# Shorter expert choice, another order of attention's steps and gates from gathered logits in a WKV and two-layer mixture-of-experts kernel

## The chip, the cores and the metric

The kernel runs on one core of a Trainium2 chip. The metric is the device time of one execution in microseconds (us); several runs are given as their median. A profile is one further execution, with every instruction's start and duration.

## The reference

Inputs are r, k, v, w of shape (2, 8, 768, 48), u, two gate matrices and two sets of expert weights (8 experts, 384x1024 and 1024x384). All arithmetic is float32.

```python
for t in range(S):                      # attention, per batch and head
    y[:, :, t] = r_t @ (state + u*k_t (x) v_t)
    state = w_t[:, None] * state + k_t (x) v_t
x = y as (1536, 384)
# layer one
logits = x @ w_gate + modality_bias[modality_id]
e = argmax(logits); gate = softmax(logits)[e]      # sum + 1e-9
x = gate * (relu(x @ w1[e]) @ w2[e])
# layer two: the same without bias; an expert takes its first 384 tokens only, others give 0
```

## The kernel before, in words

**Attention** (`attention`, L192 on) works on eight pairs of heads, i = 0 to 7, each in six chunks of 128 tokens; g = 6i + chunk counts chunks from 0 to 47. Per pair: `turn` transposes w, k, r (PE) and ACT or DVE evacuates them; `scan_s` and `scan_j` (DVE) make the decay products S and J; `mul_r` multiplies rT by J on DVE or POOL, as the string MR says by pair (L297); `uterm` and `uterm2` make the u term on POOL and DVE; `front` makes the masked scores of two chunks (PE, then `Am` on DVE, L376); `state` carries the 112x112 state: a matmul of keys and values, and then either the old state is added through the identity on PE (STATE letter p) and ACT scales (L403), or DVE adds (Z, L398) and scales (X, L401; letter v). `out_y` makes the output. The score tile in PSUM has one buffer and `Am` three.

The order is written out by hand: each engine runs its instructions in the order in which they are issued. PLAN gives, for each pair, the position (in thirds of a chunk) at which each of its steps is issued; PRE and PLAN0 do so for pair 0; FRONT, PRE, PLAN0 and END place fillers, matmuls on a constant whose result is not used (L524); XTURN, XTURN2 and XLOG place the transposes of the output and the logits of layer one; SLOT places constants, stores and the choice.

**Choice of experts** (`Pick.find`, L140 to 184). After the first batch's six chunks of logits, a count of tokens per expert is made, and the two experts with most tokens are searched, twice over with max, comparison, scan and mask. Their numbers go to registers of the SP queue, which then loads these two experts' weights. One step is issued every half chunk (`pull`), from SLOT["pick"] on. The order of the others follows (`hop`, `upto`).

**Routing** (`routing`, L771 on). From the one-hot choice of all tokens, DVE and PE make a place for every token: blocks of 256 tokens of one expert, each of two tiles of 128; `ids` and `idg` hold the token of each place. `sub`, `ex` and later `gates`, `gates1`, `gates2` (L912 to 931) make the softmax weight of each token and bring it to its place with 12 matmuls (pg, L928).

**A layer** (`moe`, L997 on) goes over the blocks. Block j gathers the rows of block j + 2 (POOL, L1046), loads the weights of block j + 2 (SP), casts the next block's weights into a high part on ACT (`hi`) and a rest on DVE (`lo`) (L1004, L1007), and runs three matmuls per product (L1080, L1115, L1128, L1146). `two` serves a block with two full tiles, `one` a block with one; which of them runs is an If on a register. In `one`, the strings of ONE say which casts and transposes are issued between the matmuls: a letter a to j is a weight piece, x and X transposes of the next block's rows, s the scaling, y, z and l the next layer's logits. In layer one each finished tile also gets its logits for layer two: with `yturn` and `ylog` in float32 for tile 0 of a two-tile block (L700, L710), and with `yturn3`, `ysplit3` and `ylog3` from three bf16 parts (L1165, L736) elsewhere. `scale` multiplies by the gate on ACT (s, L1152) or DVE (v, L1154), as SCALE says; `own` (block 0) places the rest of its weights' subtractions and the gates. `last` (L1343 on) ends layer one. The first expert of layer two is loaded ahead into the slot of the weights that is free; `p0` are the ten pieces of a layer's block 0, cast and subtracted at the layer's start. Here layer one has eight blocks (six of two tiles, two of one) and layer two ten (two, one, one, four of two, one, one, two).

## Time and profile before

| | |
|---|---|
| median of 3 runs | 474.61 us (472.51 to 476.15) |
| the profiled execution | 473.01 us |
| its span, first to last instruction | 471.3 us |
| mean granted clock of TensorE | 0.951 |
| busy, share of the span | PE 91%, PEld (weight loads) 83%, DVE 74%, ACT 51%, POOL 32% |
| attention, to the first routing | 0 to 128.8 us |
| routing and first gathers of layer one | 128.8 to 142.3 us |
| blocks of layer one | 142.3 to 290.1 us |
| end of layer one, routing of layer two | 290.1 to 308.9 us |
| blocks of layer two | 308.9 to 460.8 us |

How to read it: the profiled execution's own time is 1.7 us longer than its span. Engines are PE (TensorE), PEld (its weight loads, beside the matmuls), DVE (VectorE), ACT (ScalarE), POOL (GpSimd), SP (SyncE, which only issues transfers). A granted clock of 1.00 is the 2.4 GHz level of TensorE, 0.50 the level of 1.2 GHz. In a timeline row the bracket gives the idle time of the engine before the instruction and what ended it; x3 means three instructions in a row. Matmul ends are modelled. Instructions on one engine overlap at their ends, so a row may start before the one above it has ended.

### The profile page before, as it was taken

The page shows a single profiled execution, that of the slowest core. Times are in us where ns is not written, and L with a number is a line of the kernel's source. Part 1 is how long each engine was busy: PE and PEld are TensorE (multiplying, and loading weights), DVE is VectorE, ACT ScalarE, POOL GpSimd, SP SyncE. Part 2 cuts the span into 40 slices and gives each one's busy share as a digit, 9 for nine tenths or more (in the row PEclk, how much of TensorE's full clock was granted, in tenths as well). Part 3 has the DMA queues.
Part 4 walks back from the last instruction along what each step waited for, and adds up shares of the span by engine and source line. Part 5 has one row for each costly group of instructions (what it writes and reads, how often), then busy time and mean ns, then how long its engine had stood idle before and what let it go on. Part 6 is the DMA issues. An engine that isn't in the chain of part 4 may idle for free. (4 is left out here: it accounts for less than half of the span.)

```text
span 471.3 us, 9450 instructions
## 1 busy us (share of the span) xinstructions
PE 429.7 (91%) x3188; PEld 389.5 (83%) x3188; DVE 346.9 (74%) x669; ACT 239.4 (51%) x472; POOL 150.3 (32%) x159
## 2 busy tenths in 40 slices
PE   7989999979979899999999787898999999999990
PEld 4778878868739899999999776388899999998990
DVE  7787977994288984865947587889989559569770
ACT  3335353522344473654745464545857547568560
POOL 5528767230032032021220331243533221224500
PEclk9979999995799999999999889899999999999996
DMA  6966538108632022137772763431597676684200
GB/s 114 200 110 121 100 60 202 30 2 329 230 110 69 2 69 73 37 106 223 259 231 74 208 207 117 160 87 35 206 312 269 203 232 234 184 250 130 54 10 25
DMA packets 83989, 66.82 MB, mean 142 GB/s; under 512 B 58986, under 2 KB 76055, under 8 KB 83904
## 3 DMA queue, kind: packets, MB, share of 16 engines
q1 hardware_dynamic: 78912, 52.26, 37.4%
q0 software_dynamic: 4992, 13.53, 10.1%
q8 instruction: 42, 0.69, 0.6%
q14 instruction: 43, 0.35, 0.2%
HBM read 95.55 MB, written 11.51 MB: 227 GB/s over the span
## 5 line engine op out<-in xcount | busy, mean ns | idle before, releaser
L1007 DVE TENSOR_TENSOR w1l<-w1r,w1h 128x512 fp32r<-128x512 f32 x120 | 75.2, 683 | 0.8 <-ACT w1h L1004 0.7
L1007 DVE TENSOR_TENSOR w2l<-w2r,w2h 128x768 fp32r<-128x768 f32 x80 | 71.9, 949 | 0.7 <-ACT w2h L1004 0.5
L1004 ACT CAST w1h<-w1r 128x512 fp32r<-128x512 f32 x120 | 66.2, 621 | 7.2 <-DMA w2r<-in_moe_w_dram 6.2
L1004 ACT CAST w2h<-w2r 128x768 fp32r<-128x768 f32 x80 | 61.5, 838 | 0.0
L1133 ACT ACTIVATE qhh_m<-qh_m 128x512 fp32r<-128x512 f32 x48 | 28.7, 599 | 62.5 <-PE qh_m L1128 58.9
L1134 DVE SCALAR_TENSOR_TENSOR qhl_m<-qh_m,qhh_m 128x512 fp32r<-128x512 f32 x48 | 32.9, 686 | 28.4 <-ACT qhh_m L1133 27.8
L1128 PE MATMUL qh_m<-xh,w1h 128*128 128x256 f32 x288 | 51.6, 288 | 0.5 <-PE lpl_y_m L710 0.3
L1157 POOL DMA_INDIRECT x<-yo,ids_l x14 | 15.1, 1080 | 115.6 <-DVE yo L1154 66.0
L1128 PE MATMUL qh_m<-xl,w1h 128*128 128x256 f32 x288 | 50.2, 283 | 0.1
L1128 PE MATMUL qh_m<-xh,w1l 128*128 128x256 f32 x288 | 49.8, 282 | 0.0
L1157 POOL DMA_INDIRECT out_dram<-yo,ids_l x20 | 24.9, 1244 | 67.7 <-DVE w1l L1007 17.8
L1128 PEld LDWEIGHTS qh_m<-xh,w1h 128*128 128x128 f32 x288 | 42.3, 188 | 1.1 <-ACT xh L1337 0.8
L1046 POOL DMA_INDIRECT xg<-x,idg_l x24 | 28.1, 1170 | 45.8 <-PE xp_m L1061 32.4
L1128 PEld LDWEIGHTS qh_m<-xl,w1h 128*128 128x128 f32 x288 | 41.0, 189 | 0.5 <-DVE w2l L1007 0.5
L1128 PEld LDWEIGHTS qh_m<-xh,w1l 128*128 128x128 f32 x288 | 40.9, 188 | 0.0
L403 ACT ACTIVATE X<-endt,Sb 112x112 f32<-112x112 f32 x32 | 11.3, 354 | 50.9 <-PE endt L393 37.2
L1046 POOL DMA_INDIRECT xg<-xs,idg_l x20 | 22.7, 1136 | 34.9 <-DVE ec_l L888 29.1
L418 PE MATMUL py<-raw_v,Am 128*128 128x96 f32 x192 | 32.7, 299 | 0.0
L1062 ACT CAST xh<-xp_m 128x384 fp32r<-128x384 f32 x38 | 16.7, 485 | 27.9 <-PE xp_m L1061 26.6
L418 PEld LDWEIGHTS py<-raw_v,Am 128*128 128x128 f32 x192 | 29.5, 220 | 0.1
L1146 PE MATMUL qy_m<-w2h,qhh_m 128*128 128x384 f32 x96 | 25.6, 348 | 0.0
L1146 PE MATMUL y_m<-w2h,qhh_m 128*128 128x384 f32 x96 | 25.1, 342 | 0.0
(281 smaller groups left out, 964.7 us busy)
## 6 DMA issues: line engine op xcount, KB each, us to landing
w2r<-in_moe_w_dram SPq DMA_DIRECT2D x50, 768.0 KB
w1r<-in_moe_w_dram SPq DMA_DIRECT2D x72, 512.0 KB
xs<-zv SPq DMA_DIRECT2D x12, 192.0 KB
out_dram<-zt SPq DMA_DIRECT2D x4, 576.0 KB
raw_w<-in_w_dram SPq DMA_DIRECT2D x14, 144.0 KB
raw_r<-in_r_dram SPq DMA_DIRECT2D x14, 144.0 KB
raw_k<-in_k_dram SPq DMA_DIRECT2D x14, 144.0 KB
raw_v<-in_v_dram SPq DMA_DIRECT2D x14, 144.0 KB
```

The costliest lines, as they stand in the source:

```text
L403: nc.scalar.activation(Xn, z, AF.Identity, scale=Tn)
L418: nc.tensor.matmul(py[:, 1 - h : 4 - h : 2, 0:D], lhsT=Am[:, h], rhs=vc[:, ch, :, 0:D], start=not ch, stop=True, skip_group_check=True)
L1004: (eng.copy if eng is nc.scalar else eng.tensor_copy)(p[1], p[0])
L1007: eng.tensor_sub(p[2], p[0], p[1].bitcast(F32))
L1046: nc.gpsimd.indirect_dma_start(out=m.xg[j % 2][:, t, 0:SW], out_offset=None, in_=src, in_offset=bass.IndirectOffsetOnAxis(ap=R.idg[:, 2 * ...
L1062: nc.scalar.copy(m.xh[j % 2][:, :, ts], pt)
L1128: nc.tensor.matmul(ph[:, f], lhsT=w[s][:, kc, fs], rhs=a[s][:, kc], start=(i == 0), stop=(i == 3 * KD - 1))
L1133: nc.scalar.activation(hh, ph, AF.Relu)
L1134: nc.vector.scalar_tensor_tensor(hl, ph, 0.0, hh.bitcast(F32), ALU.max, ALU.subtract)
L1146: nc.tensor.matmul(st["y", j, t], lhsT=a[:, f, ts], rhs=w[s][:, 2 * q + f], start=(q == 0 and i == 0), stop=(q == 3 and i == 5))
L1157: nc.gpsimd.indirect_dma_start(out=dst, out_offset=bass.IndirectOffsetOnAxis(ap=R.ids[:, 2 * j + t : 2 * j + t + 1], axis=0), in_=m.yo[j % ...
```

## The change

- **Choice of experts.** `find` makes one key, 8 times the count plus the expert's number, and takes the two largest and their indices with `max` and `max_index`. It is issued from SLOT["pick"] = 32 instead of 27.
- **Attention.** All of PLAN, PRE, PLAN0, FRONT, MR, STATE, SLOT, XTURN and XTURN2 are new: STATE has p at all five places, MR gives pairs 2, 4, 5 and 6 to DVE, and the fillers are placed anew.
- **Routing.** `sub`, `ex`, `rk`, `sr` go; the place is (inc + s0) times the one-hot. The one-hot `ohp` is made in three pieces of 6, 4 and 2 columns instead of two of 6.
- **Gates.** The scratch xs gets 8 more columns, into which the logits of layer one are written; the gather brings them with the row, in layer two as before. In each block max, difference (DVE), exponential (ACT), sum and reciprocal (DVE) give the gate of its 256 places: `gates(j, 0)` and `gates(j, 1)`, issued for the next block.
- **Next logits.** Tile 0 of a two-tile block uses `yturn3`, `ysplit3`, `ylog3`; its transposes are issued one product earlier. In `one`, z and l are issued earlier.
- **Scaling** is on ACT everywhere.
- **First weights of layer two.** They are cast in the last block of layer one already, as its next block's; layer two no longer casts them again. Where the last block's number is even, `last` does it.

```diff
 WARM = (4, 12, 2, 15)
 TP = (3, 4)
+OHP = ((0, 6), (6, 10), (10, 12))
...
-PRE = ('F6', 'n0', 'w0', 'w1', 'F0', 'A', 'S0', 'J0', 'r0', 'F0', 'A', 'm0', 'k0', 'S1', 'F8', 'r1', 'F2', 'J1', 'm1', 'K0', 'F1', 'k1', 'F6')
-FRONT = {0: 3, 1: 6}
-PLAN0 = {0: ('F0', 'n1', 'K1', 'F0', 'u', 'F0'), 3: ('A',), 1: ('U',), 10: ('c0',), 14: ('c1',)}
-MR = 'vggggggg'
-STATE = 'pppvp'
+PRE = ('F6', 'n0', 'w0', 'w1', 'F5', 'A', 'S0', 'J0', 'r0', 'F0', 'A', 'm0', 'k0', 'S1', 'F5', 'r1', 'F3', 'J1', 'm1', 'K0', 'F5', 'k1', 'F0')
+FRONT = {1: 7, 13: 2, 20: 1}
+PLAN0 = {0: ('F2', 'n1', 'K1', 'F0', 'u', 'F2'), 3: ('A',), 1: ('U',), 10: ('c0',), 14: ('c1',)}
+MR = 'ggvgvvvg'
+STATE = 'ppppp'
...
-SLOT = {'consts': 21, 'small': 9, 'pick': 27, 'xs': 29, 'flag': 44}
+SLOT = {'consts': 17, 'small': 10, 'pick': 32, 'xs': 26, 'flag': 44}
...
-SCALE = 'vsv'
+SCALE = 'ssv'
...
-ONE = (('ecadfyb', '01z', 'X', '', 'lhgix', 'js'), ('badec0', 'f1h', 'xX', 'i', 'j', 'sg'))
+ONE = (('ecadfyz', '01b', 'X', 'l', 'hgixq', 'jsQ'), ('badec0', 'f1h', 'xX', 'qi', 'jQ', 'sg'))
...
+        with self.nc.allow_low_precision(reason="whole numbers up to six"):
+            ins = v.tensor_reduce(half, self.oh[:, :, 0:CH], AX.X, ALU.add)
...
+        yield v.scalar_tensor_tensor(n, pc, float(E), num, ALU.mult, ALU.add)
+        yield v.max(top, n)
+        yield v.max_index(self.index, top, n)
+        yield v.tensor_copy(self.at, self.index[0:1, 0:2])
         yield "at"
...
+        yield v.tensor_scalar(self.force, n, top[:, 1:2], None, ALU.is_ge)
         key = T("key", [P, E])
-        yield v.tensor_sub(key, b, a)
+        yield v.tensor_scalar(key, n, top[:, 0:1], None, ALU.is_equal)
+        yield v.scalar_tensor_tensor(key, n, top[:, 1:2], key, ALU.is_equal, ALU.subtract)
...
+                nc.sync.dma_start(xs.rearrange("(c p) e -> p c e", p=P)[:, cols, DM:XW], lg[:, cols])
...
-        v.tensor_sub(sub, lg, mxb)
...
-        nc.scalar.activation(ex, sub, AF.Exp)
...
-        v.tensor_mul(rk, inc, oh)
...
-            v.scalar_tensor_tensor(rk, r1, cap[:, 0:1], rk, ALU.is_le, ALU.mult)
...
-        v.tensor_reduce(sr, rk.rearrange("p e c -> p c e"), AX.X, ALU.add)
...
-        v.tensor_tensor(so, oh, s0.unsqueeze(2).to_broadcast((P, E, NC)), ALU.mult)
+        v.tensor_tensor(so, inc, s0.unsqueeze(2).to_broadcast((P, E, NC)), ALU.add)
+        v.tensor_tensor(so, so, oh, ALU.mult)
...
-        v.tensor_add(sl, sl, sr)
...
-        for h in range(2):
...
+        for a, z in OHP:
+            v.tensor_tensor(ohp[:, :, a:z], c.i1[:, :, a:z], ps_[:, a:z].unsqueeze(1).to_broadcast((P, P, z - a)), ALU.is_equal)
...
-    for p in p0:
-        hi(p, nc.scalar)
     if layer == 0:
+        for p in p0:
+            hi(p, nc.scalar)
...
+        def gates(j, part):
+
+            gd = m.gd[j % 2]
+            if part == 0:
+                lx = m.xg[j % 2][:, :, DM:XW]
+                nc.vector.tensor_reduce(m.gm[:, 0], lx, AX.X, ALU.max)
+                nc.vector.tensor_tensor(gd[:, :, 0:E], lx, m.gm[:, 0].unsqueeze(2).to_broadcast((P, 2, E)), ALU.subtract)
+                nc.scalar.activation(gd[:, :, 0:E], gd[:, :, 0:E], AF.Exp)
+            else:
+
+                nc.vector.tensor_reduce(m.gm[:, 1], gd, AX.X, ALU.add)
+                nc.vector.reciprocal(R.gate[:, 2 * j : 2 * j + 2], m.gm[:, 1])
...
-            scale(j, 1, SCALE[2])
+            scale(j, 1, "s")
...
-            if j:
+            if j or layer:
                 split(pc, 0, 2)
...
+                gates(j + 1, 0)
             second2(j, 3, 0)
             scale(j, 0, SCALE[1])
...
+            if j + 1 < NU:
+                gates(j + 1, 1)
             second2(j, 1, 1)
+            if layer == 0:
+                yturn3(j, 0)
+                ysplit3()
             second2(j, 2, 1)
-            if layer == 0:
-                yturn(j, 0)
             second2(j, 3, 1)
             if layer == 0:
-                ylog(j, 0)
-            if layer == 0:
-                scale(j, 1, SCALE[2])
+                ylog3(j, 0)
+                scale(j, 1, "s")
...
-        for i in range(6):
+        for i in range(6) if layer == 0 else ():
             lo(p0[i], nc.vector)
...
+                if j % 2 == 0:
+                    for p in p0:
+                        hi(p, nc.scalar)
+                        lo(p, nc.vector)
...
-    xs = dr.tile([N, DM], F32, name="xs")
+    xs = dr.tile([N, XW], F32, name="xs")
```

## Rows read from the trace of the kernel before

**Rows 1.** Windows: length, busy PE, PEld, DVE, ACT, POOL, granted clock, DMA share, GB/s.
```profile
22.50:26.00 3.50, 0.50 (x6) 0.21 (x5) 3.46 (x5) 0.18 (x1) 1.68 (x1) 0.91 0.79 92
26.00:32.50 6.50, 6.40 (x33) 5.77 (x33) 5.01 (x8) 2.48 (x6) 1.15 (x1) 0.52 0.63 119
32.50:100.80 68.30, 65.15 (x663) 57.21 (x662) 57.93 (x104) 33.06 (x89) 39.60 (x51) 1.00 0.45 95
100.80:104.00 3.20, 0.94 (x11) 0.61 (x9) 3.17 (x8) 0.00 (x0) 2.94 (x3) 0.98 0.00 0
104.00:124.00 20.00, 19.72 (x109) 17.69 (x110) 8.33 (x29) 5.44 (x16) 1.15 (x1) 0.50 0.75 277
```

**Rows 2.** Timeline of PE: start, duration, idle before in brackets, releaser.
```profile
24.84 0.29 PE L391 MATMUL endt<-raw_v,KT 128*48 128x48 f32 x4 [2.12 <-DVE Z L398]
...
103.10 0.71 PE L373 MATMUL pa<-rT,kT 48*128 48x128 f32 x8 [2.08 <-DVE Am L376]
```

**Rows 3.** Timeline of DVE and POOL around the second pause.
```profile
99.26 1.71 POOL L297 TENSOR_TENSOR rT<-rT,Jf 112x768 f32<-112x768 f32 x1 [6.29 <-DVE pk_mx L156]
...
99.47 1.53 DVE L158 TENSOR_TENSOR_SCAN pk_cum<-first,pk_eq 128x8 f32<-128x8 f32 x1
...
100.93 1.40 POOL L321 TENSOR_TENSOR z<-raw_r,raw_k 128x576 f32<-128x576 f32 x1
...
101.26 1.10 DVE L159 SCALAR_TENSOR_TENSOR pk_one<-pk_cum,pk_eq 128x8 f32<-128x8 f32 x1
...
102.28 0.68 DVE L376 TENSOR_TENSOR Am<-pa,mask 128x512 f32<-128x512 f32 x1
```

**Rows 4.** Groups of lines on DVE, 0 to 128 us: busy, mean ns.
```profile
L401 DVE TENSOR_SCALAR X<-Z,Sb 112x112 f32<-112x112 f32 x8 | 6.4, 804 | 0.3
...
L398 DVE TENSOR_TENSOR Z<-endt,X 112x112 f32<-112x112 f32 x8 | 2.1, 268 | 4.4 <-PE endt L391 4.4
...
L297 DVE TENSOR_TENSOR rT<-rT,Jf 112x384 f32<-112x384 f32 x2 | 1.1, 558 | 0.2
```

**Rows 5.** Timeline of PE: nine fillers, and one addition of the old state.
```profile
10.46 2.11 PE L524 MATMUL junk<-fill 128*128 128x512 bf16 x9
...
45.29 0.45 PE L393 MATMUL endt<-X,ident 112*112 112x112 f32 x2
```

**Rows 6.** Timeline of PE: matmuls of the gates, layer one, then layer two.
```profile
155.61 0.87 PE L928 MATMUL pg_m<-rg_l,ohp_l 128*128 128x78 bf16 x12 [1.13 <-DVE rg_l L924]
...
322.14 0.89 PE L928 MATMUL pg_m<-rg_l,ohp_l 128*128 128x78 bf16 x12 [1.12 <-DVE rg_l L924]
```

**Rows 7.** Timeline of one full two-tile block of layer one: PE, DVE, ACT.
```profile
208.22 0.39 PE L736 MATMUL l_y_m<-wp,yp 128*128 128x24 bf16 x9
...
218.70 0.51 PE L1146 MATMUL qy_m<-w2h,qhh_m 128*128 128x384 f32 x2
...
221.13 0.73 PE L710 MATMUL lpl_y_m<-wg,lxT_y_m 128*128 128x8 f32 x6
...
216.99 1.02 DVE L1063 TENSOR_TENSOR xl<-xp_m,xh 128x384 fp32r<-128x384 f32 x2 [0.29 <-ACT xh L1062]
...
217.85 0.58 ACT L1152 ACTIVATE yo<-qy_m,gate_l 128x384 f32<-128x384 f32 x1 [0.52 <-PE qy_m L1146]
```

**Rows 8.** Timeline of PE, DVE and ACT around a one-tile block of layer two.
```profile
432.41 0.51 PE L1080 MATMUL ph_m<-w1h,xl 128*128 128x512 f32 x1 [0.51 <-DVE w2l L1007]
...
429.67 2.68 DVE L1007 TENSOR_TENSOR w2l<-w2r,w2h 128x768 fp32r<-128x768 f32 x3
...
428.19 2.33 ACT L1004 CAST w2h<-w2r 128x768 fp32r<-128x768 f32 x3
```

**Rows 9.** Timeline of DVE: a reduction in the routing of layer two.
```profile
299.06 0.31 DVE L834 TENSOR_REDUCE sr_l<-rk_l 128x12 f32<-128x96 f32 x1
```

**Rows 10.** Timeline of POOL and PE: the gather of layer two and its first block.
```profile
304.98 1.01 POOL L1046 DMA_INDIRECT xg<-x,idg_l  x1 [0.31 <-issue]
...
308.19 0.55 PE L1336 MATMUL xp_m<-ident,xg 128*128 128x128 f32 x3 [0.71 <-DMA xg<-x,idg_l]
```

More of the change, by code (lines that the diff above doesn't have):

```diff
@@ L135, in __init__ @@
         self.T = lambda nm, shape, dt=F32: g.tile(shape, dt, name="pk_" + nm)
-        self.one = []
         self.at = self.T("at", [1, 2])
-        self.ati = self.T("ati", [1, 2], I32)
+        self.index = self.T("index", [P, 8], mybir.dt.uint32)
+        self.ati = self.index.bitcast(I32)
     def find(self):
         v, c, T = self.nc.vector, self.c, self.T
-        n = T("n", [P, E])
-        yield v.tensor_reduce(n, self.oh[:, :, 0:CH], AX.X, ALU.add)
         half = T("half", [P, E], BF16)
-        yield v.tensor_copy(half, n)
+        with self.nc.allow_low_precision(reason="whole numbers up to six"):
+            ins = v.tensor_reduce(half, self.oh[:, :, 0:CH], AX.X, ALU.add)
+        yield ins
         yield
@@ L788, in routing @@
         oh = best.oh
-        mxb = best.mx.unsqueeze(2).to_broadcast((P, NC, E))
         inc = T("inc", [P, E, NC], BF16)
@@ L910, in places @@
             v.scalar_tensor_tensor(R.tc, ti, -float(NC), R.ids, ALU.mult, ALU.add)
-        def gates():
-            yield v.tensor_reduce(se, ex, AX.X, ALU.add)
-            yield v.tensor_scalar(se, se, 1e-9, None, ALU.add)
-            yield v.reciprocal(gt, se)
-            for i in range(3):
-                yield v.tensor_copy(g3[:, :, i], gt)
-                if i < 2:
-                    yield v.tensor_sub(gt, gt, g3[:, :, i])
-        def gates1():
-            for i in range(3):
-                yield v.tensor_tensor(rg[:, :, i], ohb, g3[:, :, i].unsqueeze(2).to_broadcast((P, NC, NB)), ALU.mult)
-        def gates2(pg):
-            for col in range(NC):
-                nc.tensor.matmul(pg, lhsT=ohp[:, :, col], rhs=rg[:, col], start=(col == 0), stop=(col == NC - 1))
-            v.tensor_copy(gs, pg)
-            v.tensor_add(gs[:, 0], gs[:, 0], gs[:, 1])
-            v.tensor_add(R.gate, gs[:, 0], gs[:, 2])
-        R.control, R.places, R.gates, R.gates1, R.gates2 = control, places, gates, gates1, gates2
+        R.control, R.places = control, places
     return R
@@ L994, in __init__ @@
         self.yp = cp.tile([P, 3, KD, P], BF16, name="yp")
+        self.gd = slots("gd", [P, 2, E + 1], F32)
+        self.gm = cp.tile([P, 2, 2], F32, name="gm")
 def moe(tc, c, m, route, run, layer, src, w1d, w2d, dst, wg2, wp2, zb, following, lgs=None, psum=None, bad=None, general=None):
@@ L999, in moe @@
     n = f"_m{layer}{run}"
-    SW = XW if layer else DM
     SO = DM if layer else XW
@@ L1191, in own @@
             if k < 2:
-                for i in (6 + 2 * k, 7 + 2 * k):
+                if k == 0:
+                    gates(0, 1)
+                for i in (6 + 2 * k, 7 + 2 * k) if layer == 0 else ():
                     lo(p0[i], nc.vector)
@@ L1195, in own @@
                     load(2, (1,))
-            elif k == 2:
-                for ops in (R.gates, R.gates1):
-                    for _ in ops():
-                        pass
-            else:
-                R.gates2(psum.tile([P, 3, NB], F32, tag="tp", name="pg" + n, bufs=TP[layer]))
-                if layer == 0:
-                    R.places()
+            elif layer == 0:
+                R.places()
         def one(j, pc):
@@ L1268, in two @@
             own(j, 1)
-            if j:
+            if j or layer:
                 split(pc, 2, 6)
@@ L1277, in two @@
             own(j, 2)
-            if j:
+            if j or layer:
                 split(pc, 6, 10)
@@ L1283, in two @@
             first2(j, 3)
-            if j == 0:
+            if j == layer == 0:
                 split(pc, 6, 8)
             second2(j, 1, 0)
-            own(j, 3)
             second2(j, 2, 0)
```

57 lines of the change are left out of this document (19 added, 38 removed).

## The prediction

> **What bounds the kernel now.** I read the windows first, then the timelines of PE and DVE at the places where the windows are thin, then the groups of lines. PE is the engine that ends last nearly everywhere: in the long middle of attention it is busy 65.15 of 68.30 us at a granted clock of 1.00 [rows 1], and in the two-tile blocks of both layers its matmuls follow each other without a gap. The exceptions are what this change can win. In attention there are two pauses. At 22.5 to 26.0 PE works 0.50 of 3.50 us, and the next 6.50 us run at 0.52, about the lower level of 1.2 GHz; at 100.8 to 104.0 it works 0.94 of 3.20 us, and the next 20.00 us run at 0.50 [rows 1]. Both pauses have one shape: a first wait of 2.12 and 2.08 us for DVE, once for the state's sum Z, once for the masked scores Am [rows 2]. DVE was not short of time on average; it was held. From 99.26 POOL multiplies (rT, then z). A DVE scan over 8 columns that starts at 99.47 ends at 101.00, just behind POOL's end at 100.97, and the next small one, 101.26 to 102.36, ends with POOL's second product at 102.33; Am comes only at 102.28 [rows 3]. Those two small instructions are part of the choice of experts.
>
> **Attention.** What the two pauses cost: idle 3.50 - 0.50 = 3.0 and 3.20 - 0.94 = 2.3 us. Work at the lower level: the middle stretch does 663 matmuls in 68.30 us, 9.7 per us; 33 matmuls would take 3.4 instead of 6.5 us, and 109 would take 11.2 instead of 20.0 [rows 1]. That is 3.1 and 8.8 us. Together 17.2 us, the ceiling of what the new layout can return.
>
> The first pause goes because the fourth state of a pair is no longer summed and scaled on DVE: STATE has no v left. DVE loses eight Z and eight X, 2.1 + 6.4 us busy [rows 4]. PE gains eight additions through the identity, at most 0.45 us each and less when they overlap [rows 5]; I take 0.28, in all 2.2 us. The eight scalings go to ACT, which is busy 33.06 of 68.30 us [rows 1]. The second goes because the choice now has 6 steps up to the index instead of 17, starts five chunks later, and has done its search (max, max_index) in chunk 37, before the product of the last pair is issued to POOL in chunk 38. What is added: six more fillers net (PRE 24 for 23, FRONT 10 for 9, PLAN0 4 for none), 2.11 / 9 = 0.23 us each [rows 5], 1.3 us as a bound since some fall into waits. So 17.2 - 2.2 - 1.3 = 13.7 us at best.
>
> The new order has its own danger. Four products rT*J move from POOL to DVE, at 2 x 0.56 = 1.1 us each [rows 4]; that of pair 6 stands behind a scan and two kT and in front of the next Am. Sums of DVE durations over such four-chunk stretches come to about 9 us, against about 8 us of PE. The first chunks can wait too: its transposes use three PSUM tiles, and one is freed only behind the scan J of pair 1. New pauses can cost from nothing to the whole 17.2; I take 5.0: one pause, a little less than the smaller of the two measured ones with its slow stretch (3.0 + 3.1). Attention: -17.2 + 3.5 + 5.0 = -8.7.
>
> The Trainium skill, "SBUF — State Buffer", section "Who interferes with whom", says that a DVE instruction with two SBUF inputs contends with a GpSimd instruction that reads SBUF, and that whichever is second is fully blocked. The held scan agrees [rows 3]. The rule speaks against MR: by it each moved product can be held for a POOL product, 4 x 1.40 = 5.6 us of DVE time more; no such product beside POOL is in this trace.
>
> **Routing.** On the path from logits to indices the reduction sr and the sum sl + sr go, and one sum of inc and s0 comes; in layer two the masking of rk, another pass over 96 columns, goes too. The removed reduction takes 0.31 us [rows 9]; I price the new sum and the mask like it, so that reduction and sum cancel, the narrow sum is worth 0.2, and the one-hots in 6, 4 and 2 columns leave two matmuls behind the last piece instead of six, another 0.2. The subtraction and rk itself stand beside PE's counts and cost nothing now. So -0.4 in layer one, -0.7 in layer two; between 0 and -1.5 for both.
>
> **Gates.** The matmuls pg disappear: wait 1.13 plus 0.87 us in layer one, 1.12 plus 0.89 in layer two [rows 6]; overlapped with their neighbours 1.8 each, -3.6 in all. In their place every block gets four small DVE instructions and one exponential. I price one at 0.2 us, between nothing and the 0.31 of one over 96 columns [rows 9], nearer to the latter. In two-tile blocks DVE and ACT have room, so nothing, with two exceptions.
>
> (a) Layer one's two-tile blocks. The exponential sits on ACT in front of the scaling of yo, and waits for DVE. The two xl end at 218.01, then two small ones, the exponential and the scaling (0.58) bring yo at about 219.2; PE's transposes of yo are now one product earlier and are reached at 218.70 [rows 7]. So PE waits 0.5 us, and 0.15 more for the third part of yo before the logits. Against it the bf16 logits take 0.39 instead of 0.73 us [rows 7]. Per block between -0.35 (no wait) and +0.3; I take +0.2, times 6 is +1.2.
>
> (b) Layer two's one-tile blocks, four in two pairs. Now the casts i, j, g on ACT run from 428.19 to 430.52, their w2l on DVE from 429.67 to 432.35, and PE's second matmul of the next block starts at 432.41, right behind them [rows 8]: the same 0.05 us behind the last w2l stands in all three such exits. I read it as a wait by count: behind the If the instructions of both branches are counted from its start, and the longer branch sets the number. After the change the exponential stands before i, and waits for hl, two xl and two small ones: ACT resumes at about 430.4, and g ends near 432.7 instead of 430.5. By that count PE's first matmul, which needs xh from ACT, waits for that g, 1.2 us behind the block's end at 431.5. The scaling of the previous block now stands on ACT ahead of the casts too, and DVE carries its tail into the next block, where relu comes 0.35 us late. Worked through a pair, the end moves by 2.1 us after the old waits (0.5 and 0.2) are taken off: +4.2 for both. Without the count it is -1.4, the old waits gone; if the delays add up in DVE, +6.
>
> **Edits at nothing.** Layer two's p0 is no longer cast and subtracted: its 10 casts and first 6 subtractions lie beside routing and gathers, and the first block waits for its gather, 0.71 us to 308.19 [rows 10]; a gain of up to 1 us is possible. With that cover gone the load of block 2's weights starts earlier, beside that gather; SP has nothing else queued. I take +0.5, between 0 and +1. Logits written beside xs: four more small transfers on SP, the last behind the second w2r load; the gather that needs it also waits for the indices, which come after the whole routing. 0, at worst +3 (the time from a gather's issue, 304.98, to PE's transposes, 308.19 [rows 10]), if the transfer lands behind them. Scaling on ACT at layer one's end: in the last one-tile block the scaling is behind DVE's w2l today and would be behind the exponential then; 0, between -1.5 and +0.8.
>
> **The sum.** -8.7 - 1.1 - 3.6 + 1.2 + 4.2 + 0.5 = -7.5. The profiled execution took 473.01 us (span 471.3), so 465.5; the median of the runs shown, 474.61, is 1.6 above it, so 467.1.
>
> **Rivals.**
> 1. Both pauses go and none comes, and the exits of one-tile blocks don't wait: -13.7 for attention, and -1.1 - 3.6 + 1.2 + 0.5 = -3.0 for the layers, 457.9. For it: the search no longer meets POOL's products. Against it: DVE's fuller stretches.
> 2. The second pause stays, shifted: Am still behind a scan and POOL. Then attention has 3.0 + 3.1 - 3.5 = -2.6, in all -1.4, 473.2. For it: the scan J, two kT, the search and Am still follow each other on DVE within three chunks. Against: no small two-input instruction is in front of the critical Am while POOL works.
> 3. Slower. The four DVE products make pauses of their own: each like the first (2.3 idle and 3.1 slow), one like the second (2.3 + 8.8). Three of them give 11.1 + 2 x 5.4 = 21.9, attention +8.2, in all +9.4: 484.0. It decides from the third such pause on; with two, 16.5, the time is about 478.6. For it: 1.1 us on a DVE that is busy 57.93 of 68.30 us [rows 1]. Against: 8.5 us of states leave DVE at the same time. The rule quoted above would be its mechanism.
>
> **How the numbers follow.** Forecast 0.42, rival 1 0.20, rival 2 0.25, rival 3 0.13. A measurement of this kernel tells about 1% from no change, 4.7 us. Faster by more: forecast and rival 1, 0.62; within: rival 2, 0.25; slower: 0.13. The range 458 to 478 takes in rival 1, rival 2, the bounds of (a) and (b), and leaves out rival 3's full price and the last of the ceiling. The forecast's own range is 462 to 471.
>
> **What would show it.** Right: attention's end moves from 128.8 to about 120 us, and the windows up to it show no long stretch at 0.5; no pg matmuls; L710 only in the last step; PE waits of 0.5 us before the transposes of yo in layer one, and of about 1.2 us at the exits of layer two's one-tile blocks. Wrong: a stretch at 0.5 in attention longer than 6 us, a wait of PE for Am or kT above 2 us, or exits without a wait.

## The result, and the profile after

The changed kernel takes 467.62 us (median of 4 runs, 466.87 to 467.75), the kernel before 475.31 us beside it (4 runs, 472.51 to 476.15). The ratio is 0.9845, with a 95% interval from 0.9801 to 0.9889: a gain of 1.5%. The profiled execution took 467.6 us, its span is 465.9 us, 5.4 less than the 471.3 of before. One of the 42 runs of the kernel before took 462.37 us at a mean granted clock of 0.981, the others 467.92 to 479.03 us; no profile of that run was kept, so how much of the gain hangs on the long stretches at the lower clock, which the profiled execution had, stays open.

The forecast was 467.1 us. Its total came out, but not its terms: two misses of opposite sign cancelled, which is luck. The table below gives the stages in us, each cut at a row of PE's timeline: attention ends with PE's last transpose of the logits; routing ends with the first matmul of layer one's first block; the two-tile blocks end with the first matmul of the first one-tile block (the exit between them is thus in their stage); layer one ends with its last product; "between" ends with the first matmul of layer two; layer two ends with its last product. e1, e6 and f1 are experiments told below.

| stage | before | after | forecast change | measured change | e1 | e6 | f1 |
|---|---|---|---|---|---|---|---|
| attention, to its end | 128.8 | 112.1 | -8.7 | -16.7 | 113.3 | 112.3 | 112.6 |
| routing, layer one | 13.5 | 13.3 | -0.4 | -0.2 | 14.0 | 13.4 | 13.6 |
| two-tile blocks, layer one | 120.6 | 128.6 | -1.8 + 1.2 | +8.0 | 121.1 | 122.0 | 119.8 |
| one-tile blocks, layer one | 27.1 | 27.5 | 0 | +0.4 | 24.8 | 28.1 | 26.1 |
| between the layers | 18.8 | 22.8 | -0.7 | +4.0 | 19.8 | 21.2 | 19.3 |
| layer two | 151.4 | 149.8 | -1.8 + 4.2 + 0.5 | -1.6 | 153.3 | 149.9 | 149.9 |
| tail | 11.0 | 11.8 | 0 | +0.8 | 12.2 | 11.9 | 12.0 |
| span | 471.3 | 465.9 | -7.5 | -5.4 | 458.5 | 458.9 | 453.3 |

So attention gave back 8 us more than forecast, and the three stages from layer one's blocks to layer two lost 12.4 us, where the forecast had -1.3. These are the windows of the changed kernel that answer to [rows 1]; the columns are the same, and the last window ends with attention, at 112.

```profile
22.50:26.00 3.50, 3.19 (x31) 2.86 (x28) 3.20 (x6) 1.87 (x5) 1.68 (x1) 1.00 0.77 101
26.00:32.50 6.50, 6.21 (x64) 5.30 (x64) 6.32 (x11) 4.05 (x10) 1.73 (x2) 1.00 1.07 201
32.50:100.80 68.30, 67.23 (x688) 59.33 (x688) 54.51 (x101) 34.89 (x96) 36.23 (x50) 1.00 0.49 115
100.80:104.00 3.20, 3.20 (x35) 2.78 (x33) 2.88 (x10) 1.30 (x5) 0.96 (x3) 1.00 1.07 402
104.00:112.00 8.00, 7.08 (x76) 5.53 (x78) 1.81 (x8) 3.21 (x12) 0.00 (x0) 1.00 0.84 310
```

Both pauses are gone, the granted clock is 1.00 throughout, and in the long middle window PE has also gained: 67.23 us busy and 688 matmuls where it had 65.15 and 663. That part was not in the forecast's ceiling. Before had small waits between its two pauses and behind the second, which I had not added up. Here are four of them, from PE's timeline of the kernel before:

```profile
50.45 0.71 PE L373 MATMUL pa<-rT,kT 48*128 48x128 f32 x8 [0.62 <-POOL rT L297]
51.89 0.45 PE L393 MATMUL endt<-X,ident 112*112 112x112 f32 x2 [0.50 <-DVE X L401]
...
61.65 0.44 PE L451 MATMUL xt<-ident,zv 128*128 128x128 f32 x2 [0.78 <-DVE kT L270]
...
104.28 0.40 PE L391 MATMUL endt<-raw_v,KT 128*48 128x48 f32 x4 [0.46 <-DVE Z L398]
```

They come to 2.4 us, and in the changed kernel no wait of PE in attention is above 0.40 us from 13 us on.

Now a two-tile block of layer one, to be held against [rows 7]. The lines are from the timelines of PE, DVE and ACT of the changed kernel; the first three are from its first block.

```profile
142.55 0.55 PE L1140 MATMUL yt_m<-ident,yo 128*128 128x128 f32 x3 [0.89 <-ACT yo L1127]
146.26 0.24 PE L730 MATMUL l_y_m<-wp,yp 128*128 128x24 bf16 x3 [1.00 <-DVE yp L1146]
147.86 0.82 PE L1103 MATMUL qh_m<-xh,w1h 128*128 128x256 f32 x3 [0.77 <-PE l_y_m L730]
...
186.34 0.55 PE L1140 MATMUL yt_m<-ident,yo 128*128 128x128 f32 x3 [0.22 <-ACT yo L1127]
188.82 0.51 PE L730 MATMUL l_y_m<-wp,yp 128*128 128x24 bf16 x9
190.08 0.60 PE L1103 MATMUL qh_m<-xh,w1h 128*128 128x256 f32 x3 [0.74 <-ACT yo L1127]
...
188.48 0.56 DVE L1147 TENSOR_TENSOR yp<-yr_m,yp 128x384 bf16<-128x384 f32 x1
...
189.02 0.58 ACT L1127 ACTIVATE yo<-qy_m,gate_l 128x384 f32<-128x384 f32 x1 [1.55 <-PE qy_m L1121]
```

A full block takes 20.4 us (169.7 to 190.1) where it took 19.2 to 19.3. The wait that the prediction looked for is there, before the transposes of yo, but it is 0.22 us, not 0.5. The larger one stands at the end of the block, 0.74 us before the next block's first matmul, where the prediction had none. The second block takes 21.9 us. It starts at the lower level of the clock, as this window shows (columns as in [rows 1]):

```profile
147.90:151.00 3.10, 3.10 (x15) 3.10 (x16) 0.00 (x0) 0.00 (x0) 2.28 (x3) 0.52 0.20 73
```

In the 3.4 us before it, among the waits shown of the first block, PE had worked 1.27 us. In e2 below PE had worked 0.95 of 3.06 us at the same place, the granted clock stayed at 1.00, and the second block takes 20.4 us like the others. So about 1.5 us of this stage are the clock.

Between the layers the profile shows waits that it can put down to nothing ("issue"): two on DVE, one on ACT, and PE behind them.

```profile
284.12 0.48 ACT L696 COPY lxT_y_m<-lpt_y_m 128x384 f32<-128x384 f32 x1 [1.90 <-issue]
...
285.87 0.33 DVE L1328 TENSOR_SCALAR sp_m<-i,tp_l 128x128 f32<-128x128 f16 x1 [2.86 <-issue]
...
290.97 0.25 DVE L753 TENSOR_REDUCE mx_l<-lg 128x12 f32<-128x96 f32 x1 [3.18 <-issue]
...
292.71 0.17 PE L790 MATMUL pc_l<-inc_l,blk 128*128 128x8 bf16 x1 [2.88 <-DVE inc_l L784]
```

In the kernel before, the instruction that is L1328 here (L1352 there) waited 0.83 us, put down to the scaling on DVE ahead of it, and the reduction of L753 (L759 there) did not wait:

```profile
293.10 0.34 DVE L1352 TENSOR_SCALAR sp_m<-i,tp_l 128x128 f32<-128x128 f16 x1 [0.83 <-DVE yo L1154]
...
295.76 0.25 DVE L759 TENSOR_REDUCE mx_l<-lg 128x12 f32<-128x96 f32 x1
```

In layer two, the waits at its one-tile blocks, of PE's timeline, and ACT's last casts ahead of the first exit, to be held against [rows 8]:

```profile
332.98 0.47 PE L1055 MATMUL ph_m<-w1h,xh 128*128 128x512 f32 x1 [0.45 <-ACT w2h L964]
339.12 0.77 PE L1074 MATMUL hp_m<-ident,h_m 128*128 128x128 f32 x4 [0.56 <-DVE h_m L1067]
...
425.44 0.50 PE L1055 MATMUL ph_m<-w1h,xl 128*128 128x512 f32 x1 [0.41 <-DVE w2l L967]
431.39 0.77 PE L1074 MATMUL hp_m<-ident,h_m 128*128 128x128 f32 x4 [0.60 <-DVE h_m L1067]
...
331.31 2.29 ACT L964 CAST w2h<-w2r 128x768 fp32r<-128x768 f32 x3
```

The two waits at an exit (for w2h and w2l) are 0.45 and 0.41 us, where 1.2 was forecast and where the exits of before had 0.55 and 0.51. The other two, 0.56 and 0.60 us for h on DVE, stand inside the block and are new.

### The profile page after: what moved, and what is told of

It is laid out like the page before. It is cut to its first block, busy times and chain, and to the rows that moved or that the text cites. A ratio compares the mean times of both kernels' runs of the same rounds, so it can differ in the third digit from the quotient of the medians.

```text
span 465.9 us, 9517 instructions
## 1 busy us (share of the span) xinstructions
PE 422.4 (91%) x3199; PEld 379.9 (82%) x3204; DVE 332.1 (71%) x685; ACT 247.2 (53%) x506; POOL 155.9 (33%) x157
## 5 line engine op out<-in xcount | busy, mean ns | idle before, releaser
L967 DVE TENSOR_TENSOR w1l<-w1r,w1h 128x512 fp32r<-128x512 f32 x114 | 71.5, 684 | 8.6 <-ACT w1h L964 8.4
L967 DVE TENSOR_TENSOR w2l<-w2r,w2h 128x768 fp32r<-128x768 f32 x76 | 68.6, 951 | 7.7 <-ACT w2h L964 7.5
L1132 POOL DMA_INDIRECT x<-yo,ids_l x14 | 30.0, 2145 | 107.7 <-ACT yo L1127 30.4
L964 ACT CAST w1h<-w1r 128x512 fp32r<-128x512 f32 x114 | 62.8, 619 | 0.9 <-DVE yo L731 0.6
L964 ACT CAST w2h<-w2r 128x768 fp32r<-128x768 f32 x76 | 58.2, 832 | 0.0
L1008 POOL DMA_INDIRECT xg<-x,idg_l x24 | 26.6, 1110 | 63.8 <-DVE gate_l L1038 34.6
L1103 PEld LDWEIGHTS qh_m<-xh,w1l 128*128 128x128 f32 x288 | 41.5, 191 | 0.0
L1024 ACT CAST xh<-xp_m 128x384 fp32r<-128x384 f32 x38 | 16.7, 485 | 43.1 <-PE xp_m L1023 37.2
L395 ACT ACTIVATE X<-endt,Sb 112x112 f32<-112x112 f32 x40 | 14.1, 353 | 38.0 <-PE endt L385 27.1
L1008 POOL DMA_INDIRECT xg<-xs,idg_l x20 | 22.0, 1100 | 27.1 <-DVE ec_l L868 18.3
L410 PE MATMUL py<-raw_v,Am 128*128 128x96 f32 x192 | 28.5, 271 | 0.0
L410 PEld LDWEIGHTS py<-raw_v,Am 128*128 128x128 f32 x192 | 25.4, 191 | 0.1
L1025 DVE TENSOR_TENSOR xl<-xp_m,xh 128x384 fp32r<-128x384 f32 x38 | 19.6, 550 | 8.2 <-ACT xh L1024 8.1
```

The source lines that it names most:

```text
L395: nc.scalar.activation(Xn, z, AF.Identity, scale=Tn)
L410: nc.tensor.matmul(py[:, 1 - h : 4 - h : 2, 0:D], lhsT=Am[:, h], rhs=vc[:, ch, :, 0:D], start=not ch, stop=True, skip_group_check=True)
L964: (eng.copy if eng is nc.scalar else eng.tensor_copy)(p[1], p[0])
L967: eng.tensor_sub(p[2], p[0], p[1].bitcast(F32))
L1008: nc.gpsimd.indirect_dma_start(out=m.xg[j % 2][:, t], out_offset=None, in_=src, in_offset=bass.IndirectOffsetOnAxis(ap=R.idg[:, 2 * j + t ...
L1024: nc.scalar.copy(m.xh[j % 2][:, :, ts], pt)
```

## Experiments

Times are medians, with the range of the runs; the kernel before ran beside each group. "After" is the changed kernel, at 467.62 us.

**Attention alone (e1).** The kernel before with attention's constants of the change and its class Pick, all else as before:

```diff
-STATE = 'pppvp'
+STATE = 'ppppp'
-MR = 'vggggggg'
+MR = 'ggvgvvvg'
...
```

> The kernel before with only the attention part of the change: its constants (PLAN, PRE, FRONT, PLAN0, MR, STATE, SLOT, XTURN, XTURN2) and the short choice of experts; gates, routing, logits and layer two's first weights as before. Theory A: attention's end moves as in the changed kernel, from 128.8 to about 112 us, and everything behind it is as before, so the time falls by 16.7 us, to about 458.6 us (ratio 0.965); the rest of the change then costs about 9 us. Theory B: part of the 16.7 us is only passed on (loads or gathers that the end of attention now meets), and the time falls by 8 to 12 us only. The prediction's term for this part was -8.7 us.

Measured: 463.68 us (460.27 to 467.0, 4 runs; before beside it 473.25), span of the profiled run 458.5. By the stages (column e1) attention ends at 113.3, 15.5 us earlier, as theory A says. The time doesn't fall by as much: 9.6 us between the medians, 12.8 us in the span, which is nearer to theory B. The code behind attention is that of before, and yet its stages differ from before by -2.3 (one-tile blocks) to +1.9 us (layer two); differences of this size in one profiled run say little about a change. In the profiled runs the rest of the change costs 7.4 us net: 465.9 less 458.5. The medians say 3.9 us; e1's runs scatter more. The forecast of -8.7 for attention was too small for its end.

**What in attention does it (e4, e9, e10, e11).** e4 keeps the short choice and takes back all nine of attention's constants; e9, e10 and e11 each take back one thing in the changed kernel:

```diff
e9:  -STATE = 'ppppp'
     +STATE = 'pppvp'
e10: -SLOT = {..., 'pick': 32, ...}    class Pick as changed
     +SLOT = {..., 'pick': 27, ...}    class Pick as before
e11: -MR = 'ggvgvvvg'
     +MR = 'vggggggg'
```

> The changed kernel with attention's constants of before (PLAN, PRE, FRONT, PLAN0, MR, STATE, SLOT, XTURN, XTURN2), the short choice of experts kept. Theory A: the second pause of before was made by the long choice beside POOL, so the short choice alone removes it (2.3 us idle and 8.8 us at the lower clock) and only the first pause is back: 467.6 + 3.0 + 3.1, about 474 us (ratio 0.997). Theory B: the second pause belongs to the old layout (products, scans and turns in the same chunks), and both pauses are back: about 484 us (ratio 1.02).

> The changed kernel with the state of the fourth chunk of each pair summed and scaled on DVE again (STATE as before). Theory A, the prediction's: the first pause of before came from that sum; it is back, near 24 us (2.1 us idle for Z, 0.97 for X, and some us at the lower clock), and attention ends 3 to 6 us after the 112.1 us of the changed kernel, with six more such pairs that may add up to 2 us each. Theory B: the new order leaves room for it, and attention ends by 113 us. The profile decides: attention's end.

> The changed kernel with the long choice of experts of before, started in the chunk in which it started before (27). Theory A, the prediction's: the long choice beside POOL's products makes the second pause; masked scores are late near 100 us, PE waits about 2 us, up to 9 us run at the lower clock, and attention ends at 114 to 123 us. Theory B: with the new order of products and scans the long choice fits in as well, and attention ends at 112 to 113 us; then it is the layout, not the shorter choice, that took the pause away. The profile decides: attention's end and the clock after 90 us.

> The changed kernel with the four moved products rT*J back on POOL (MR as before), all else of the new order kept. Theory A: the products on POOL were part of what made before late (its first waits in the middle of attention name POOL's rT, and a product takes 1.41 us there against 0.95 us for the pair on DVE, behind others); attention then ends 3 to 9 us after the 112.1 us of the changed kernel, which is what is left of the gain when the state's 6.2 us and the choice's 1.8 us are taken off. Theory B: the order alone carries the rest, and attention ends by 113 us; then nothing is gained by the move, and nothing lost by what the prediction feared of it. The profile decides: attention's end.

Measured, end of attention: e4 132.8 us, e9 118.3, e10 113.9, e11 113.4, after 112.1. Times: e4 483.7 us (481.38 to 488.55); the others had one run each (474.76, 476.49, 473.07), and their verdict is read from attention alone. PE's timeline of e4:

```profile
25.29 0.29 PE L383 MATMUL endt<-raw_v,KT 128*48 128x48 f32 x4 [2.12 <-DVE Z L390]
26.55 0.72 PE L385 MATMUL endt<-X,ident 112*112 112x112 f32 x2 [0.97 <-DVE X L393]
...
80.00 0.77 PE L365 MATMUL pa<-rT,kT 48*128 48x128 f32 x8 [1.36 <-POOL rT L289]
...
107.12 0.72 PE L365 MATMUL pa<-rT,kT 48*128 48x128 f32 x8 [0.76 <-DVE Am L368]
...
109.51 0.29 PE L383 MATMUL endt<-raw_v,KT 128*48 128x48 f32 x4 [1.67 <-DVE Z L390]
```

And of e9:

```profile
24.36 0.29 PE L383 MATMUL endt<-raw_v,KT 128*48 128x48 f32 x4 [1.32 <-DVE Z L390]
25.62 0.71 PE L385 MATMUL endt<-X,ident 112*112 112x112 f32 x2 [0.97 <-DVE X L393]
```

The first pause is the state on DVE: e9 brings it back, at the same place and with the same two releasers, and costs 6.2 us. The second pause is not the long choice alone. In e10 the long choice, started in its old chunk, fits into the new order: 1.8 us, no stretch below full clock up to the end of attention. In e4 the short choice, also from its old chunk, does not save the old order: the second pause is there, 0.76 us for Am and 1.67 for the state's sum Z (2.08 and 0.46 before), a product on POOL makes another, and attention ends 4.0 us later than in the kernel before. Moving the four products gives 1.3 us (e11). The kernels with attention as changed end it between 111.9 and 112.6 us, e1 at 113.3, so the 1.3 and 1.8 us are small; the 6.2 us are not. State, choice and products together are 9.3 of the 16.7 us; the rest lies in the order itself or in how these work together, and the order alone was not tried.

**The end of a two-tile block (e2, e5, e6).** e2 puts the last scaling back on DVE; e5 moves the exponential behind the scaling; e6 makes the logits in float32 as before, their transposes one product later, with the last scaling on DVE:

```diff
e2:
                 ylog3(j, 0)
-                scale(j, 1, "s")
+                scale(j, 1, "v")
e5:
-                gates(j + 1, 0)
             second2(j, 3, 0)
             scale(j, 0, SCALE[1])
+            if j + 1 < NU:
+                gates(j + 1, 0)
e6:
+            second2(j, 2, 1)
             if layer == 0:
-                yturn3(j, 0)
-                ysplit3()
-            second2(j, 2, 1)
+                yturn(j, 0)
             second2(j, 3, 1)
             if layer == 0:
-                ylog3(j, 0)
-                scale(j, 1, "s")
+                ylog(j, 0)
+                scale(j, 1, "v")
```

> The changed kernel with one letter changed: the scaling of the second tile at the end of layer one's two-tile blocks goes back from ACT to DVE. Theory A: each of these blocks now ends with a 0.74 us wait of PE for that scaling on ACT, and it goes; six blocks, -4.4 us against the changed kernel, about 463.2 us (ratio 0.974). Theory B: the wait moves to DVE, which then carries the scaling ahead of its casts' remainders of the next block, and the time stays at 467.6 us.

> The changed kernel with the exponential of the gates (and the two small DVE instructions ahead of it) moved behind the scaling of the first tile in two-tile blocks. In layer one each such block takes 20.35 us where it took 19.3: PE waits 0.22 us ahead of yo's transposes, and 0.74 us at the block's end. Theory A: both waits hang on one chain (the exponential waits 1.0 us for DVE, the scaling stands behind it, then transposes, three parts, logits); PE's last wait of the block, for the third part, ends too late for the block's exit to be passed in time. With the scaling about 0.9 us earlier both waits go: -0.9 x 6 = -5.4 us, about 462.2 us. Theory B: the 0.74 us are the exit itself, which the short bf16 matmuls at the end can't cover, whenever they start: only the 0.22 us go, -1.3 us, about 466.3 us.

> The changed kernel with the next logits of the first tile in layer one's two-tile blocks made as before: transposes of yo one product later, logits in float32, the second tile's scaling on DVE at the end. Theory A: what makes these blocks 1.05 us longer is the chain of the three parts at their end; without it 6 x 1.05 = -6.3 us, and 1.1 us less at the first exit to a one-tile block: about 460.2 us. Theory B: it is the exponential or the gates on ACT, and the blocks stay near 20.3 us: 467.6 us.

Measured: e2 467.96 us (465.8 to 470.49), no gain; e5 466.05 (465.06 to 471.94), ratio to before 0.9832 (0.9775 to 0.989); e6 459.52 (457.72 to 463.1), ratio 0.9707 (0.9624 to 0.9791), 8.1 us better than after (1.4% by the two ratios to the kernel before beside each). The blocks' ends on PE and DVE, first e2:

```profile
191.31 0.60 PE L1103 MATMUL qh_m<-xh,w1h 128*128 128x256 f32 x3 [0.76 <-PE l_y_m L730]
```

Then e5:

```profile
191.56 0.56 DVE L1147 TENSOR_TENSOR yp<-yr_m,yp 128x384 bf16<-128x384 f32 x1
...
193.18 0.60 PE L1103 MATMUL qh_m<-xh,w1h 128*128 128x256 f32 x3 [0.77 <-ACT yo L1127]
```

And e6:

```profile
203.59 0.73 PE L704 MATMUL lpl_y_m<-wg,lxT_y_m 128*128 128x8 f32 x6
204.17 0.61 PE L1103 MATMUL qh_m<-xh,w1h 128*128 128x256 f32 x3
```

The releaser that the profile names in the changed kernel, the scaling on ACT, is not the cause: in e2 there is no such scaling, and the wait is the same. In the changed kernel DVE's third part of yo ends at 188.48 + 0.56 = 189.04, and the next block starts 1.04 us later; in e5 it ends at 192.12, and the next block starts 1.06 us later. With the float32 logits there is no third part, and the next block follows at once. So the cause lies in how these logits are made: e6 takes it away, and e2 shows that the scaling is not the part of e6 that does it. How it costs 1 us is argued only. The chain from the transposes through the third part takes 189.04 - 186.34 = 2.7 us in the changed kernel, and behind the transposes PE has only two products, 2.2 us, to do; that explains 0.5 us at most. Moving the exponential shortens a block by 0.4 us (19.95 for 20.4), not by 0.9: the transposes are then reached without a wait, but no sooner than PE comes to them, and the wait at the end stays (0.77). That is theory B of e5: the stage is 1.2 us shorter, 1.3 were expected. Whether the 1.05 us behind the last part is the exit of the block or the short matmuls themselves stays open. e6's full blocks take 19.3 to 19.6 us, about as before: its theory A holds, -6.6 in the stage, although its exit to the one-tile blocks was longer (below).

**The one-tile blocks (e7).**

```diff
-ONE = (('ecadfyz', '01b', 'X', 'l', 'hgixq', 'jsQ'), ...
+ONE = (('ecadfyb', '01z', 'X', 'l', 'hgix', 'jsqQ'), ...
```

> The changed kernel with another order in layer one's one-tile blocks: the last two parts of yo behind the DVE half of relu again (as before), and the exponential behind the last cast and the scaling. Theory A: the waits of PE in the second of these blocks (0.79 us for h on ACT, 1.87 us for h on DVE) come from the two parts ahead of relu's half and from ACT's wait of 2.04 us for DVE ahead of the exponential; they go, and with them the stretch at 0.91 of the clock (1.8 us): -2.7 to -4.5 us, about 464 us. Theory B: DVE is behind anyway in these blocks because of the exit before them (3.79 us), and the time stays at 467.6 us.

Measured: 472.12 us (467.89 to 475.63, 10 runs), ratio 0.9946 (0.9908 to 0.9984). The 1.87 us for h on DVE is gone, but PE waits 1.59 us for h on ACT instead (ACT's scaling waits for the end of the block, and the casts of the next stand behind it): one-tile stage 27.9 us, after 27.5. A miss: no gain. The profiled run is slower than after by its other stages: the exit to the first one-tile block takes 6.30 us, and routing 16.1 us. The exits, from the timelines of ACT and PE, first of the kernel before:

```profile
259.98 2.70 ACT L1004 CAST w1h<-w1r 128x512 fp32r<-128x512 f32 x5 [0.66 <-issue]
...
262.94 0.47 PE L1080 MATMUL ph_m<-w1h,xh 128*128 128x512 f32 x1 [2.52 <-ACT w1h L1004]
```

Of the changed kernel:

```profile
249.84 0.58 ACT L1127 ACTIVATE yo<-qy_m,gate_l 128x384 f32<-128x384 f32 x1 [1.55 <-PE qy_m L1121]
250.98 2.70 ACT L964 CAST w1h<-w1r 128x512 fp32r<-128x512 f32 x5 [0.56 <-DVE yo L731]
...
253.95 0.76 PE L1055 MATMUL ph_m<-w1h,xh 128*128 128x512 f32 x1 [3.79 <-DVE w1l L967]
```

Of e2, whose last scaling of a two-tile block is on DVE as before:

```profile
250.21 2.70 ACT L964 CAST w1h<-w1r 128x512 fp32r<-128x512 f32 x5 [0.66 <-DVE yr_m L1143]
...
254.91 0.47 PE L1055 MATMUL ph_m<-w1h,xh 128*128 128x512 f32 x1 [3.47 <-DVE w1l L967]
```

Of e7, with one of its windows (DMA share in the last column but one) and the instruction queues in that window:

```profile
255.07 2.70 ACT L964 CAST w1h<-w1r 128x512 fp32r<-128x512 f32 x5 [0.55 <-DVE yo L731]
...
260.56 0.77 PE L1055 MATMUL ph_m<-w1h,xh 128*128 128x512 f32 x1 [6.30 <-issue]
...
257.60:258.60 1.00, 0.00 (x0) 0.00 (x0) 1.00 (x3) 0.17 (x1) 0.69 (x2) 0.65 0.99 308
...
q14 instruction: 2, 0.02, 11.0%
q8 instruction: 1, 0.02, 5.8%
```

Before and after, PE starts 2.96 and 2.97 us behind the start of ACT's five casts. With the scaling last on ACT these casts start 0.8 us behind PE's end, where they had started 0.4 us ahead of it, and the two waits differ by 1.27 us. That looks like the scaling's price, but e2 speaks against it: with the scaling back on DVE the casts start 1.2 us ahead of PE's end, and PE still waits 3.47 us, 0.95 of the 1.27 us more than before, and starts 4.7 us behind the casts. In e7 PE starts 5.5 us behind the casts, with the DMA engines full and instructions being loaded in the middle of the wait.

**Between the layers (e3, e8).** e3 takes out instructions that do not run with these inputs (those behind an even last block). e8 moves a load of 1.5 MB:

```diff
e3:
-                if j % 2 == 0:
-                    for p in p0:
-                        hi(p, nc.scalar)
-                        lo(p, nc.vector)
e8:
         st["k"] = kind(0)
+        if layer == 1:
+            m.raw.load(1, w1d, w2d, slice(EXPERT0[1], EXPERT0[1] + 1), parts=(1,))
...
-                er = EXPERT0[j % 2]
-                m.raw.load(j % 2, *following, slice(er, er + 1), parts=(1,))
```

> The changed kernel without the instructions that part layer two's first weights behind an even last block. With these inputs the last block is odd, so none of the removed instructions runs. Theory A: the pauses between the layers that the trace puts down to nothing (2.86 and 3.18 us on DVE, 1.90 us on ACT) come from the longer code that lies between the branches, and they go: -4 to -6 us against the changed kernel, about 462.5 us (ratio 0.973). Theory B: they come from something else (the order of what does run), and the time stays at 467.6 us.

> The changed kernel with the load of 1.5 MB of layer two's second weights moved from the end of layer one to behind layer two's first register load, so that it starts about 15 us later. Theory A: the pauses that the trace puts down to no releaser (2.86 and 3.18 us on DVE, 1.90 us on ACT) are instructions that are being fetched over the same DMA engines as this load; without it they fall to about the 0.8 us of the kernel before: -4 us, and perhaps +1 for the load beside layer two's first gathers: about 464 us. Theory B: the pauses belong to the jump past the code alone and stay; 467.6 us or a little more.

Measured: e3 468.15 us (464.64 to 469.29), e8 471.15 (467.4 to 473.51, 10 runs), ratio 0.9927 (0.9888 to 0.9967). Neither gains. DVE's timeline of e3:

```profile
290.34 0.33 DVE L1328 TENSOR_SCALAR sp_m<-i,tp_l 128x128 f32<-128x128 f16 x1 [5.56 <-issue]
```

And of e8:

```profile
288.70 0.34 DVE L1330 TENSOR_SCALAR sp_m<-i,tp_l 128x128 f32<-128x128 f16 x1 [2.67 <-issue]
...
291.30 0.25 DVE L753 TENSOR_REDUCE mx_l<-lg 128x12 f32<-128x96 f32 x1 [0.61 <-DVE lg L1341]
```

In e3 the reduction of L753 does not wait. The code in the branch that is not taken is not the cause of the first wait, and the load is not either: without it the wait is 2.67 us, with the DMA engines 4% busy. What e8 saves at the second it loses later: PE waits 3.29 us for a gather of layer two that now meets the load.

**Together (f1).** e6, and in addition:

```diff
-SCALE = 'ssv'
+SCALE = 'vsv'
-ONE = (('ecadfyz', '01b', 'X', 'l', 'hgixq', 'jsQ'), ...
+ONE = (('ecadfyb', '01z', 'qX', 'l', 'hgix', 'Qjs'), ...
...
-    raw.second()
...
                 nc.sync.dma_start(xs.rearrange("(c p) e -> p c e", p=P)[:, NC - LAST :, DM:XW], lg1[:, NC - LAST :])
+                raw.second()
```

> The changed kernel with what the runs so far point to: layer one's two-tile blocks make their logits in float32 as before, with the second tile's scaling on DVE; its one-tile blocks have yo's last parts behind relu's DVE half again, the scaling on DVE, and the exponential early in the block, where its inputs have long been there; and the 1.5 MB load behind attention is issued after the last logits' store instead of ahead of it. Theory A: two-tile stage about 121 us (128.6 in the changed kernel), one-tile stage about 25 (27.5), routing of layer one 13.3 us in every run, the path between the layers about 20 (22.8): a span near 453 us, so about 455 us. Theory B: the gates themselves make the one-tile blocks longer wherever they stand (28.1 us in the run with float32 logits), and the span stays near 458 us, about 459.5 us.

Measured: 455.63 us (454.34 to 456.57, 6 runs; before beside it 472.73), ratio 0.9658 (0.9613 to 0.9703). It is 12.0 us faster than the changed kernel (1.9% by the two ratios): the gates from gathered logits, the short routing and layer two's weights are kept, and most of what was lost in layer one is back. Theory A, but the one-tile stage stays at 26.1 us rather than 25. At the exit PE waits 2.87 us. DVE of f1, between the layers:

```profile
276.59 0.33 DVE L1327 TENSOR_SCALAR sp_m<-i,tp_l 128x128 f32<-128x128 f16 x1 [1.88 <-issue]
```

With the 0.61 us of scaling last on DVE, as before, the wait at the first is 1.88 us, and "between" is 19.3 us.

## Why the prediction was right in the total and not in its terms

- **Attention, -8.7, measured -16.7.** The step that failed is "I take 5.0" for new pauses: no wait of PE above 0.40 us came. The ceiling of 13.7 failed too: it counted the two pauses and left out the small waits between them; with the 2.4 us shown of these it is 17.2 + 2.4 - 3.5 = 16.1, near the 16.7 measured. The first pause was explained rightly (e9). The second was not: I put it down to the small instructions of the choice beside POOL, and in e4, with the short choice in the old layout, it is there at almost the same length, while e10 does without it with the long choice in the new one. Which part of the layout makes it stays open. Whether the 2.2 and 1.3 us of added work on PE were paid can't be read from these runs.
- **The moved products.** The forecast took from them a danger, and rival 3 its price. They take 0.95 us for a whole product in all four places, and attention has no pause at them. The Trainium skill, "SBUF — State Buffer", section "Who interferes with whom", has the rule that the second of two such instructions is held. One of the four met a product of POOL, and there it was POOL that came second. Timelines of DVE and POOL of the changed kernel:

```profile
33.22 0.95 DVE L289 TENSOR_TENSOR rT<-rT,Jf 112x768 f32<-112x768 f32 x1
...
31.88 1.41 POOL L313 TENSOR_TENSOR z<-raw_r,raw_k 128x576 f32<-128x576 f32 x1
33.37 2.07 POOL L314 TENSOR_TENSOR z<-z,ub 128x576 f32<-128x576 f32 x1
```

  POOL's product z<-z,ub took 2.07 us where it takes 1.40 or 1.41 for six of the other pairs, and no wait of PE followed. The trace agrees with the rule; I had assumed that DVE would be the one held.
- **Routing, -0.4 in layer one, measured -0.2.** The edit that I cost at nothing, "0, at worst +3", is the logits written beside xs. In some runs the stage is longer by about that much: in e2, e5, e7, e8, e10 and e11, where nothing of routing was changed, the stage takes 15.4 to 16.9 us. In e7 the first gather is issued at 122.49 us, in the changed kernel at 120.09, with the indices ready at the same time. That small transfer stands behind 1.5 MB of weights on SP's queue. f1 issues it ahead of them and shows 13.6 us, but e3, e4, e6 and e9 show 13.4 to 13.7 without that; so that this transfer is the cause is argued, not shown. In layer two, "-0.7" did not come: from the end of inc to the end of the last matmul of pid it takes 6.04 us, 5.69 before. There 12 fillers at a granted clock of 0.50 take 5.28 us, and pid stands behind them on PE.
- **The matmuls pg, -1.8 a layer.** They are gone. Layer two's first block takes 17.8 us where it took 20.7. In layer one the gain is hidden by (a): the first block takes 22.5 us, 21.6 before, but 20.0 in e6 and f1.
- **(a), +0.2 a block, measured about +1.0.** The step that failed is "between -0.35 (no wait) and +0.3". The wait at the transposes was priced (0.5, measured 0.22), what follows to the block's end was not: I added "0.15 more for the third part" and had no term for 0.63 to 0.74 us ahead of the next block's first matmul. e6 shows that they come with these logits. Of the 8.0 us in this stage, full blocks are 3.1, the first two 3.4 (with waits of 0.89, 1.00 and 0.77 us in the first and about 1.5 us by the clock in the second), the last with its exit 1.5.
- **(b), +4.2, measured +2.1.** The one-tile blocks of layer two took 41.5 us in four and take 43.6. The direction was right and the path only in part. ACT's delay is there: its last casts start 1.2 us ahead of PE's end (331.31 to 332.53; 1.1 by the forecast), where before they started 3.3 us ahead. The step that failed is "PE's first matmul, which needs xh from ACT, waits for that g, 1.2 us behind the block's end": PE starts at 332.98, and the casts end at 333.60. The exits wait no longer than before. What came is the late relu, 0.56 and 0.60 us for h on DVE where the forecast had 0.35.
- **Scaling on ACT at layer one's end, "0, between -1.5 and +0.8".** At the exit to the one-tile blocks 1.27 us were lost, and between the layers 4.0, but the runs do not show the scaling as the cause. e2 still has 0.95 of the 1.27 us. Between the layers e2 and e9, which scale the one-tile blocks on ACT like the changed kernel, lose 0.7 and 0.9 us, e5 5.2; the second wait, 3.18 us in the changed kernel, is there in e5 and not in e2 and e9. f1 has this scaling back on DVE and loses 0.5 us, with other edits too. What failed is that the forecast had no term for the waits at these branches.
- **The sum.** The terms missed by -8.0 in attention and by about +10 behind it, and that these cancelled is luck. Rival 1 was nearer in attention (-13.7) and wrong in the layers; rivals 2 and 3 did not occur.

## What to carry to other kernels

The first pause was worth what the windows said (6.1 us, 6.2 by e9), but the ceiling of a new order has to include the small waits of the same kind. When a step is put at the end of a loop body or a branch, price everything up to the next body's first matmul, the exit included, and hold it against the work that PE still has behind it: here 1 us was paid in every block. Take the releaser that a profile names as a lead: e2 removed it, and the wait stayed. And undo each half of a change that "gained": here attention alone took 12.8 us off the span, and the other half had given 4 (medians) to 7 us (profiles) back.

## What was not expected of the hardware

The waits told here stand where an engine leaves a branch. At the same place between the layers they last 1.17 us (e1), 1.88 (f1), 2.67 (e8), 2.86 (after) and 5.56 (e3), put down to "issue", where before had 0.83 put down to DVE's scaling; at the exit to the one-tile blocks PE waits 2.5 to 6.3 us. The profile puts some waits inside blocks down to "issue" too (on ACT 4.02 us at 266.69 in the kernel before), so the name alone proves nothing. The trace has DMA queues of kind "instruction", and in most kernels a few of their packets fall into these waits; in e7 they do so while the DMA engines are 99% busy, mostly with weights. The Trainium skill, "Runtime: NRT & Kernel Launch", section "Instruction fetch mechanics", says that a taken branch to code that is not at hand makes the engine wait for a DMA fetch. The trace agrees as far as it goes. At the exit to the one-tile blocks the wait goes with the DMA engines' busy share during it, in all 14 kernels: 2.52 to 2.87 us at 0.22 (before, e1, f1, with no instruction packet in the wait), 3.28 to 3.79 at 0.45 to 0.67 (nine kernels, e2 among them), 4.74 and 6.30 at 0.97 and 0.96 (e6, e7), whether the scaling before it is on ACT or on DVE. That a full DMA makes the wait longer is what this suggests; no run here shows it by itself, between the layers e8 has 2.67 us at 0.04, and the second wait of 3.18 us came in some kernels (after, e5, e7, e10, e11) and not in others (e2, e3, e4, e6, e9) without a change to what stands there. Where these differences come from stays open.
